# Joining the first-pass weights of layer one from a float16 copy and one shift

## The chip, the core and the metric

The kernel runs on one core of one Trainium2 chip. The engines of that core work at the same time, each through its own list of instructions in order: TensorE (PE, and PEld for its weight loads), VectorE (DVE), ScalarE (ACT), GpSimd (POOL) and SyncE (SP), whose queue issues nearly all DMAs here. They wait for each other through semaphores. The metric is the device time of one execution in microseconds.

## The reference, cut to what matters

Attention over 4 batches with 8 heads, 576 positions and head size 64 (four heads see a local window of 32, four a strided pattern), then two dense layers on the 2304 rows of 512 values:

```python
x = attention(q, k, v)                      # (2304, 512)
r = maximum(x @ moe_w_in, 0)                # (2304, 2048)
x = (s * (r * r) + b) @ moe_w_out           # (2304, 512)
h = x @ moe2_w_in
out = ((h * cos(h)) @ moe2_w_out).astype(float32)
```

The weights come as float64. The chip's engines don't compute in that format, so the kernel takes each weight apart by its bits: it reads the two 32-bit words of a float64, builds a float32 from them, and splits that into a rounded part (hi) and a rest (lo), since TensorE multiplies the format float32r and three products (hi by hi, hi by lo, lo by hi) stand for one float32 product.

## The kernel before

**Stages.** From the start to about 155 us the kernel computes the attention, batch by batch, and beside it the first of two "plain" passes of layer one (PASSES = (5, 3): five chunks of 128 hidden columns, then three). From then on come the second pass and the products of both layers in blocks, up to the end.

**Attention.** A batch is five pairs of heads (two local, two strided, one "rem" for what is left over). For each pair TensorE forms the scores (L649, into `s_ps`; for the first two batches the mask is added by L642), VectorE takes the maximum (L663) and scales it (L665), ScalarE forms the exponentials (L670, four for each of the two halves j), VectorE normalises (L681, L682 and L683, into `part`), TensorE transposes (L696, `t_ps`), ScalarE copies (L707), TensorE multiplies by the values (L742, `o_ps`), and the result is split on ScalarE (L166, `xhi`) and VectorE (L171, `xlo`). In batches after the first, GpSimd does the small L665 and L681. Runs of products into `dummy` (L775) keep TensorE busy while the first pairs go through.

**The first pass.** The functions `mm_h` and `mm_2` multiply x by chunk n of the first weights (`h_ps`, L928), and, after the activation on ScalarE and VectorE (L951 to L957, split into `gh`, `gl`), by chunk n of the second ones (`acc`, L928). A weight chunk (n, k) must be converted first: k is 0 for the first weights and 1 for the second.

**Conversion of the first five chunks.** These ten tiles of 128 x 512 float64 weights are loaded early by `w_early_load` (L299) into the buffers `wearly`, issued from SP's queue between the loads of q, k and v; a buffer that a converted tile has left takes the next tile (`w_next_load`). `convert_ops` gives the list of steps: four on VectorE into the float32 tile `wtmp` (L178 scales the high word, L252 shifts it by 3, L254 ors in the top of the low word, L259 ors in the sign), then the hi part on ScalarE (`w<-wtmp`, L166) and the lo part on VectorE (`w<-wtmp,w`, L171). `bg_step` takes 1.8 steps of that list per step of the attention. The chunks of the second pass (`wraw`, L342) go the same way but have L178's step on ScalarE (L176). All weights that come later in the kernel are converted in another way, by `to_f32`: ScalarE copies the top 16 bits as float16 into `consts` (L200) and VectorE joins them with bits 16 to 47 in one instruction (L201).

**What sets the order.** The Python code gives one program order; a scheduler then places each engine's instructions by the times at which it expects their inputs to be ready, and keeps a few pairs apart where the code says so. So a conversion with fewer steps moves its neighbours on several engines.

Of the kernel before, what the change touches and what calls it, by code (L numbers as in the profile page):

```python
# [9 lines left out]
F32 = mybir.dt.float32  # L10
F32R = mybir.dt.float32r
BF16 = mybir.dt.bfloat16
U32 = mybir.dt.uint32
U16 = mybir.dt.uint16
F16 = mybir.dt.float16
AF = mybir.ActivationFunctionType
ALU = mybir.AluOpType
# [5 lines left out]
P = 128  # L23
NC = DM // P
NF = DFF // P
# [21 lines left out]
FP = PASSES[0]  # L47
# [84 lines left out]
def net(ctx, tc, qkl, qks, rqk, vloc, vstr, rv, wi1, wo1, wp1, wo2, wp2, s, b, out):  # L132
    nc = tc.nc
    wi_raw = wi1.bitcast(U32)
    wo_raw = [x.bitcast(U32) for x in (wo1, wo2)]
    wp_raw = [x.bitcast(U32) for x in (wp1, wp2)]

    const = ctx.enter_context(tc.tile_pool(name="const", bufs=1))
    wp = ctx.enter_context(tc.tile_pool(name="wp", bufs=1))
# [4 lines left out]
    h_p = ctx.enter_context(tc.tile_pool(name="hs", bufs=3))  # L144
# [11 lines left out]
    identb = constb[:, :P]  # L156
    mloc = constb[:, P : P + 4 * LK].rearrange("p (n k) -> p n k", n=4)
    mrem = constb[:, P + 4 * LK :].rearrange("p (n k) -> p n k", n=4)
    sb = const.tile([P, 32], F32, name="sb")
    xhi = const.tile([P, NC, NT], F32R, name="xhi")  # L160
    xlo = const.tile([P, NC, NT], F32R, name="xlo")
    part_p = ctx.enter_context(tc.tile_pool(name="part", bufs=1))
# [2 lines left out]
    def split_hi(dst_hi, src, scale=1.0):  # L165
        nc.scalar.activation(dst_hi, src, AF.Copy, scale=scale)  # L166

    def split_lo(dst_lo, src, hi, scale=1.0):
        if scale != 1.0:
            return nc.vector.scalar_tensor_tensor(dst_lo, src, scale, hi.bitcast(F32), ALU.mult, ALU.subtract)  # L170
        return nc.vector.tensor_tensor(dst_lo, src, hi.bitcast(F32), ALU.subtract)  # L171


    def rebias(t, h, on_act):
        if on_act:
            nc.scalar.activation(t, h.bitcast(F32), AF.Copy, scale=2.0**-112)  # L176
        else:
            nc.vector.tensor_scalar(t, h.bitcast(F32), 2.0**-112, None, ALU.mult)  # L178
# [42 lines left out]
    class Raw:  # L221


        def __init__(self, tile, src):
# [7 lines left out]
            else:  # L232
                self.words = tile[:, :1024]
                nc.sync.dma_start(out=self.words, in_=src)

    wtile, ready = {}, set()
    converted = [None]

    def convert_ops(raws, dst, key):

        tmp = st_p.tile([P, 512], F32, tag="st", name="wtmp")
        ops = []
        o = 0
        on_act = key[0] >= FP
        for raw in raws:
            n = raw.shape[1]
            t = tmp[:, o : o + n]
            tu = t.bitcast(U32)
            lo32, hi32 = raw[:, :, 0], raw[:, :, 1]
            o += n  # L250
            ops.append(lambda t=t, h=hi32: rebias(t, h, on_act))
            ops.append(lambda tu=tu: nc.vector.tensor_scalar(tu, tu, 3, None, ALU.logical_shift_left))  # L252
            ops.append(
                lambda tu=tu, l=lo32: nc.vector.scalar_tensor_tensor(  # L254
                    tu, l, 29, tu, ALU.logical_shift_right, ALU.bitwise_or
                )
            )
            ops.append(
                lambda tu=tu, h=hi32: nc.vector.scalar_tensor_tensor(  # L259
                    tu, h, 0x80000000, tu, ALU.bitwise_and, ALU.bitwise_or  # L260
                )
            )
        ops.append(lambda: split_hi(dst[:, 0, :], tmp))

        def last():
            converted[0] = split_lo(dst[:, 1, :], tmp, dst[:, 0, :])

        if key[0] < 2:
            ops += [lambda: None] * 3
        ops.append(last)  # L270
        ops.append(lambda: ready.add(key))
        if key in raw_at:
            ops.append(lambda: w_next_load(key))
        return ops

    def w_src(n, k, c0, c1):
        src = wo_raw[n // NF][n % NF] if k else wi_raw[n]
        return src[:, 2 * c0 : 2 * c1].rearrange("p (c t) -> p c t", t=2)
# [14 lines left out]
    raws, raw_at = {}, {}  # L293
    to_load = [(n, k) for n in range(2, FP) for k in range(2)]

    def w_early_load(n, k, at):
        raw_at[n, k] = at
        raws[n, k] = raw = wp.tile([P, 512, 2], U32, name="wearly", **at)
        nc.sync.dma_start(out=raw, in_=w_src(n, k, 0, 512))  # L299

    def w_next_load(key):

        if to_load and key != (1, 1):
            w_early_load(*to_load.pop(0), raw_at[key])
# [32 lines left out]
    def w_job(n, k):  # L337

        raws = []
        for c in range(2):  # L340
            raw = st_p.tile([P, 256, 2], U32, tag="st", name="wraw")
            nc.sync.dma_start(out=raw, in_=w_src(n, k, 256 * c, 256 * (c + 1)))  # L342
            raws.append(raw)
        return convert_ops(raws, w_alloc(n, k), (n, k))
# [666 lines left out]
    nc.vector.memset(zeros, 0.0)  # L1011
    warm = zeros.bitcast(BF16)
    nc.vector.memset(sb, 0.0)
    nc.scalar.activation(sb[:, 2:3], sb[:, 3:4], AF.Exp)
    make_identity(nc, ident)
    def keep(m, base, pattern, cm):
# [28 lines left out]
    for what, *arg in FIRST:  # L1045
        if what == "w":
            w_early_load(*arg, dict(tag="w15", bufs=1) if arg[1] else buf0())
        else:
            {"qk": load_qk, "v": load_v, "rq": load_rem_qk, "rv": load_rem_v}[what](0, *arg)

    for n, k in BG_ORDER:
        bg.append(lambda n=n, k=k: convert_ops([raws.pop((n, k))], w_alloc(n, k), (n, k)))
# [3 lines left out]
    while not att.batch_done(0):  # L1056
        next(steps)
        tick()
        if att.n == 3 and (1, 1) not in raws:
            for n, k in SECOND:  # L1060
                w_early_load(n, k, dict(tag="w14", bufs=1))
            nc.sync.dma_start(out=sb[:, 0:1], in_=s.partition_broadcast(P))
            nc.sync.dma_start(out=sb[:, 1:2], in_=b.partition_broadcast(P))
        if normed[0] is not None and (bg_now or att.n >= EARLY_AT[len(BG_ORDER) - len(bg)]):
            prev = converted[0] or normed[0]
            with tc.issue_after(normed[0].ins), tc.issue_after(prev.ins):
                bg_step(EARLY_BG)
        if early < 2 and att.pairs[PRE // 2 + early].stored:
            mm_h(0, early)
            early += 1  # L1070
# [50 lines left out]
    for i in range(14):  # L1121
        k, cp, prev = RING[i % 12]
# [30 lines left out]
    class Temp:  # L1153
# [8 lines left out]
        def set(self, x, y, op=ALU.subtract):  # L1162
            def at(z, i):
                if isinstance(z, Temp):
                    return z.ms[i][1] if len(z.ms) == len(self.ms) else z.ms[0][1][:, self.ms[i][0], :]
                return z[:, self.ms[i][0], :]

            for i, (_, t) in enumerate(self.ms):
                nc.vector.tensor_tensor(t, at(x, i), at(y, i), op)  # L1169
                yield  # L1170
# [101 lines left out]
    for u_, (ly, s_, p) in enumerate(UNITS[:NU2]):  # L1272
        for f in range(2):
# [4 lines left out]
            key = u_, f  # L1278
            if held.get(b_, (None,))[0] == (ly, p):
                key = held[b_][1]  # L1280
# [653 lines left out]
    for u in range(NU2 + 2):  # L1934
# [15 lines left out]
        hs = {}  # L1950
# [165 lines left out]
```

## Time and profile before

| | us |
|---|---|
| Median of 3 runs | 829.58 |
| Lowest and highest | 829.22, 830.01 |
| The profiled execution | 829.99 |
| Span of its trace | 828.2 |
| Busy: PE | 814.7 |
| Busy: DVE | 639.1 |
| Busy: ACT | 588.9 |

The profiled execution is 0.41 us above the median, and 1.8 us of it lie outside the span of the trace. A row of the trace names a line of the kernel, an engine, an operation and its tiles (result<-inputs). "Idle before" is the time in which an engine had nothing running, and the arrow behind it names what ended that wait. Where the engine waited for nothing that the profile shows, the word there is "issue".

### The profile page before, as it was taken

The page shows a single profiled execution, that of the slowest core. Times are in us where ns is not written, and L with a number is a line of the kernel's source. Part 1 is how long each engine was busy: PE and PEld are TensorE (multiplying, and loading weights), DVE is VectorE, ACT ScalarE, POOL GpSimd, SP SyncE. Part 2 cuts the span into 40 slices and gives each one's busy share as a digit, 9 for nine tenths or more (in the row PEclk, how much of TensorE's full clock was granted, in tenths as well). Part 3 has the DMA queues.
Part 4 walks back from the last instruction along what each step waited for, and adds up shares of the span by engine and source line. Part 5 has one row for each costly group of instructions (what it writes and reads, how often), then busy time and mean ns, then how long its engine had stood idle before and what let it go on. Part 6 is the DMA issues. An engine that isn't in the chain of part 4 may idle for free.

```text
span 828.2 us, 15435 instructions
## 1 busy us (share of the span) xinstructions
PE 814.7 (98%) x5545; PEld 731.2 (88%) x5545; DVE 639.1 (77%) x1209; ACT 588.9 (71%) x1237; POOL 20.5 (2%) x74
## 2 busy tenths in 40 slices
PE   8899999999999999999999999999999999999998
PEld 5676777889888999899999999898899999999998
DVE  6898866877668569976766787877758999578985
ACT  7888877668767677777678666667568765589753
POOL 3120000000000000000000000000000000000000
PEclk9999999999999999999999999999999999999999
DMA  9755542587688988996889989899797878974675
GB/s 336 231 192 169 160 125 85 196 287 244 245 306 297 359 313 287 331 322 222 306 290 376 327 290 359 306 307 384 250 351 260 273 251 259 290 251 151 210 248 179
DMA packets 102269, 220.00 MB, mean 266 GB/s; under 512 B 9136, under 2 KB 53424, under 8 KB 102192
## 3 DMA queue, kind: packets, MB, share of 16 engines
q1 hardware_dynamic: 100464, 211.83, 75.0%
q10 hardware_dynamic: 1728, 7.18, 2.6%
q8 instruction: 44, 0.72, 0.3%
q14 instruction: 33, 0.27, 0.1%
HBM read 163.92 MB, written 55.05 MB: 264 GB/s over the span
## 4 chain that ended last, share of the span: by engine, by line
PE 77%; DVE 7%; ACT 2%; issue 1%; DMA 1%; ACTq 0%; DVEq 0%
PE acc L1872 10%; PE acc L928 9%; PE pb L1982 9%; PE pa L1982 9%; PE h_ps L928 9%; PE acc L1681 8%; PE acc L1862 7%; PE acc L1551 6%; PE pa L1551 3%; PE pb L1551 3%; DVE graw L1142 2%; DVE xlo L171 2%; PE pa L1681 1%; PE pb L1681 1%; DVE xt L1169 1%
## 5 line engine op out<-in xcount | busy, mean ns | idle before, releaser
L928 PE MATMUL h_ps<-xhi,w 128*128 128x512 f32 (+1 forms) x320 | 100.9, 377 | 0.2
L928 PE MATMUL acc<-gh,w 128*128 128x512 f32 (+1 forms) x320 | 99.1, 374 | 0.0
L1872 PE MATMUL acc<-gh,w2l 128*128 128x512 f32 (+1 forms) x384 | 84.9, 336 | 0.0
L1982 PE MATMUL pb<-xhi,wfl 128*128 128x384 f32 x268 | 80.1, 339 | 0.4 <-DVE h L1962 0.2
L1982 PE MATMUL pa<-xhi,wfl 128*128 128x384 f32 x268 | 79.6, 337 | 0.0
L166 ACT ACTIVATE xhi<-graw 128x384 fp32r<-128x384 f32 (+1 forms) x84 | 51.3, 629 | 38.4 <-DVE graw L1142 18.3
L928 PEld LDWEIGHTS h_ps<-xhi,w 128*128 128x128 f32 x320 | 58.5, 189 | 11.8 <-ACT w L166 1.1
L928 PEld LDWEIGHTS acc<-gh,w 128*128 128x128 f32 x320 | 58.4, 189 | 10.2 <-ACT gh L166 0.2
L1681 PE MATMUL acc<-xhi,w2m 128*128 128x384 f32 x256 | 67.1, 334 | 0.0
L1872 PEld LDWEIGHTS acc<-gh,w2l 128*128 128x128 f32 x384 | 59.7, 188 | 7.6 <-DMA w2l<-w2s 0.4
L1419 ACT ACTIVATE h<-h 128x768 f32<-128x768 f32 x48 | 40.3, 840 | 29.2 <-DVE h L1962 28.9
L171 DVE TENSOR_TENSOR xlo<-graw,xhi 128x384 fp32r<-128x384 f32 (+1 forms) x84 | 55.0, 686 | 7.5 <-ACT xhi L166 7.5
L1862 PE MATMUL acc<-w2l,gh 128*128 128x512 f32 x192 | 59.7, 390 | 0.0
L928 PE MATMUL h_ps<-xlo,w 128*128 128x512 f32 (+1 forms) x160 | 59.4, 371 | 0.0
L928 PE MATMUL acc<-gl,w 128*128 128x512 f32 (+1 forms) x160 | 59.3, 371 | 0.0
L1551 PE MATMUL acc<-xhi,wfl 128*128 128x384 f32 x196 | 55.2, 335 | 0.1
L171 DVE TENSOR_TENSOR gl<-r,gh 128x512 fp32r<-128x512 f32 (+2 forms) x56 | 40.6, 725 | 16.1 <-ACT gh L1419 8.7
L1982 PEld LDWEIGHTS pb<-xhi,wfl 128*128 128x128 f32 x268 | 49.4, 188 | 3.5 <-DVE h L1962 1.0
L1982 PEld LDWEIGHTS pa<-xhi,wfl 128*128 128x128 f32 x268 | 49.4, 188 | 1.7 <-ACT q L1994 0.4
L1872 PE MATMUL acc<-gl,w2l 128*128 128x512 f32 x192 | 49.0, 335 | 0.0
L1681 PEld LDWEIGHTS acc<-xhi,w2m 128*128 128x128 f32 x256 | 46.4, 188 | 0.0
L1982 PE MATMUL pb<-xlo,wfl 128*128 128x384 f32 x134 | 45.0, 336 | 0.0
(248 smaller groups left out, 2087.4 us busy)
## 6 DMA issues: line engine op xcount, KB each, us to landing
wfl<-wfb SPq DMA_DIRECT2D x68, 512.0 KB, 5.1
wfl<-wfa SPq DMA_DIRECT2D x34, 512.0 KB, 5.7
w2l<-w2s SPq DMA_DIRECT2D x28, 512.0 KB, 5.8
praw<-in_wp_dram SPq DMA_DIRECT2D x22, 512.0 KB, 4.8
oraw<-in_wo_dram SPq DMA_DIRECT2D x22, 512.0 KB, 4.8
w2m<-wsum SPq DMA_DIRECT2D x22, 512.0 KB, 3.8
wfb<-ob SPq DMA_DIRECT2D x21, 512.0 KB, 4.3
w2s<-ow SPq DMA_DIRECT2D x20, 512.0 KB, 4.4
```

The source lines that it names most:

```text
L166: nc.scalar.activation(dst_hi, src, AF.Copy, scale=scale)
L171: return nc.vector.tensor_tensor(dst_lo, src, hi.bitcast(F32), ALU.subtract)
L928: nc.tensor.matmul(*args, **kw)
L1142: return nc.vector.tensor_tensor(d, x, y, op)
L1169: nc.vector.tensor_tensor(t, at(x, i), at(y, i), op)
L1419: return nc.scalar.activation(*args, **kw)
L1551: nc.tensor.matmul(self.bank(v, bi), a, b[:, m, :], start=st and m == 0 and i == 0, stop=m == 1 and i == 2, skip_group_check=True)
L1681: nc.tensor.matmul(self.acc(j, e), w[u][:, wi, c], g[:, u], start=first and i == 0, stop=last and i == 2, skip_group_check=True)
L1862: nc.tensor.matmul(accs[e], g[:, e * P : (e + 1) * P], w[:, wi, :], start=start and i == 0, stop=stop and i == 2, skip_group_check=True,)
L1872: nc.tensor.matmul(o, w[:, wi, e * P : (e + 1) * P], g[:, c : c + o.shape[1]], start=start and i == 0 and (c == 0 or e % 2 == 0), stop=sto ...
L1982: nc.tensor.matmul(pb[bi], a, b[:, m, :], start=st and m == 0 and i == 0, stop=m == 1 and i == 2, skip_group_check=True)
```

## The change

The ten tiles of the first pass's weights now go the way of `to_f32`, but with both steps on VectorE. The load puts the 4,096 bytes of a partition's row at 2 bytes past the buffer's start, so that bits 16 to 47 of every float64 form an aligned 32-bit word. The first new step multiplies the top 16 bits, read as bfloat16, by 0.5 and writes them as float16 into the upper halves of a new tile `tops`, whose lower halves stay zero; the second shifts the middle word right by 13 and ors the two. The value so made is a 256th of the weight, and the factor 256 goes into the two splits, which were plain before. `tops` is one buffer of the pool `hs`, cleared once at the start; `sb` shrinks from 32 to 8 columns. The number of entries in the list stays (two of them do nothing now).

```diff
-    sb = const.tile([P, 32], F32, name="sb")
+    sb = const.tile([P, 8], F32, name="sb")
...
+    tops = h_p.tile([P, 512], F32, tag="hs", name="tops")
...
+        scale = 1.0
+        if key[0] < FP:
+            raw, scale = raws[0], 256.0
+            halves, middles = raw.bitcast(BF16)[:, 4:2052:4], raw[:, 1:1025:2]
+            ops += [
+                lambda: nc.vector.tensor_scalar(tops.bitcast(F16)[:, 1::2], halves, 0.5, None, ALU.mult),
+                lambda: nc.vector.scalar_tensor_tensor(
+                    tmp.bitcast(U32), middles, 13, tops.bitcast(U32), ALU.logical_shift_right, ALU.bitwise_or
+                ),
+                lambda: None,
+                lambda: None,
+            ]
+            raws = []
...
-        ops.append(lambda: split_hi(dst[:, 0, :], tmp))
+        ops.append(lambda: split_hi(dst[:, 0, :], tmp, scale))
...
-            converted[0] = split_lo(dst[:, 1, :], tmp, dst[:, 0, :])
+            converted[0] = split_lo(dst[:, 1, :], tmp, dst[:, 0, :], scale)
...
-        raws[n, k] = raw = wp.tile([P, 512, 2], U32, name="wearly", **at)
-        nc.sync.dma_start(out=raw, in_=w_src(n, k, 0, 512))
+        raws[n, k] = raw = wp.tile([P, 1026], U32, name="wearly", **at)
+        nc.sync.dma_start(out=raw.bitcast(U16)[:, 1:2049], in_=(wo_raw[n // NF][n % NF] if k else wi_raw[n]).bitcast(U16))
...
+    nc.vector.memset(tops, 0.0)
```

The change moves instructions up to about the end of the third batch's first pairs; behind that, all engines have the same order as before. In the rows that follow, lines of the new kernel are up to 15 higher: L677, L679, L684, L695, L696, L697, L710, L721, L942 are L663, L665, L670, L681, L682, L683, L696, L707, L928 of before, and its L251 and L252 are the two new steps.

VectorE in the attention of the first batch, at the conversion of the second tile, before. `sm` holds the maxima and sums, `part_99` the exponentials of a strided pair; `s_ps` and the last two `sm` belong to the "rem" pair:

```order
L254 SCALAR_TENSOR_TENSOR wtmp<-wearly,wtmp 128x512
L683 TENSOR_TENSOR part_99<-part_99,sm 128x256
L681 TENSOR_SCALAR sm<-sm 128x4
L663 TENSOR_REDUCE sm<-s_ps 128x4
L682 RECIPROCAL sm<-sm 128x4
L663 TENSOR_REDUCE sm<-s_ps 128x4
L683 TENSOR_TENSOR part_99<-part_99,sm 128x256
L259 SCALAR_TENSOR_TENSOR wtmp<-wearly,wtmp 128x512
L171 TENSOR_TENSOR xlo<-o_ps,xhi 128x18x12 x2
L665 TENSOR_SCALAR sm<-sm 128x4 x2
```

The same place on VectorE now:

```order
L252 SCALAR_TENSOR_TENSOR wtmp<-wearly,tops 128x512
L695 TENSOR_SCALAR sm<-sm 128x4
L696 RECIPROCAL sm<-sm 128x4
L697 TENSOR_TENSOR part_99<-part_99,sm 128x256
L695 TENSOR_SCALAR sm<-sm 128x4
L677 TENSOR_REDUCE sm<-s_ps 128x4
L696 RECIPROCAL sm<-sm 128x4
L677 TENSOR_REDUCE sm<-s_ps 128x4
L697 TENSOR_TENSOR part_99<-part_99,sm 128x256
L679 TENSOR_SCALAR sm<-sm 128x4 x2
```

The last joining step and the two `xlo` splits no longer stand between the maxima and their scaling. ScalarE a little later, before; the eight exponentials of `part_99` are those of the "rem" pair, `w_534` is the hi part of the second tile:

```order
L166 ACTIVATE xhi<-o_ps 128x18x12 x2
L166 ACTIVATE w_534<-wtmp 128x512
L707 ACTIVATE part_98<-t_ps 128x512
L670 ACTIVATE part_99,sm<-s_ps,sm 128x64 x8
L670 ACTIVATE part_98,sm<-s_ps,sm 128x96 x2
```

The same place on ScalarE now; the first eight exponentials of `part_99` in this piece are the "rem" pair's:

```order
L166 ACTIVATE w_534<-wtmp 128x512
L684 ACTIVATE part_99,sm<-s_ps,sm 128x64
L166 ACTIVATE xhi<-o_ps 128x18x12 x2
L684 ACTIVATE part_99,sm<-s_ps,sm 128x64 x2
L721 ACTIVATE part_98<-t_ps 128x512
L684 ACTIVATE part_99,sm<-s_ps,sm 128x64 x5
L684 ACTIVATE part_98,sm<-s_ps,sm 128x96 x4
```

The hi part has moved ahead of the `xhi` splits; of the "rem" pair's exponentials one now stands ahead of those splits, and two more ahead of the copy of the transposes. TensorE after the first batch, before; `w_534` and `w_661` are the first weights of chunk 1 and the second weights of chunk 0, `part_99` an attention pair of the second batch:

```order
L928 MATMUL h_ps<-xhi,w_534 128x512 x2
L928 MATMUL h_ps<-xlo,w_534 128x512
L928 MATMUL h_ps<-xhi,w_534 128x512
L696 MATMUL t_ps<-consts,part_99 96x128 x4
L928 MATMUL acc<-gh,w_661 128x512 x4
L696 MATMUL t_ps<-consts,part_99 96x128 x4
L928 MATMUL acc<-gl,w_661 128x512
```

The same place on TensorE now; `w_853` are the first weights of chunk 2:

```order
L942 MATMUL h_ps<-xhi,w_534 128x512
L942 MATMUL h_ps<-xlo,w_534 128x512
L942 MATMUL h_ps<-xhi,w_534 128x512 x2
L942 MATMUL h_ps<-xlo,w_534 128x512
L942 MATMUL h_ps<-xhi,w_534 128x512
L942 MATMUL h_ps<-xhi,w_853 128x512
L942 MATMUL h_ps<-xlo,w_853 128x512
L942 MATMUL h_ps<-xhi,w_853 128x512
L710 MATMUL t_ps<-consts,part_99 96x128 x4
L942 MATMUL h_ps<-xhi,w_853 128x512
L942 MATMUL h_ps<-xlo,w_853 128x512
L710 MATMUL t_ps<-consts,part_99 96x128 x4
```

The products of chunk 2 now stand ahead of the transposes of that pair and of the first products into `acc`.

## Rows read from the trace of the kernel before

**Rows 1.** The page: busy time by engine, and shares of the chain of waits.

```profile
PE 814.7 (98%) x5545; PEld 731.2 (88%) x5545; DVE 639.1 (77%) x1209; ACT 588.9 (71%) x1237; POOL 20.5 (2%) x74
...
PE 77%; DVE 7%; ACT 2%; issue 1%; DMA 1%; ACTq 0%; DVEq 0%
```

**Rows 2.** Windows: stretch, length, busy us (instructions) by engine, granted clock, DMA share, GB/s.

```profile
10.00:33.00 23.00, 19.74 (x404) 13.86 (x402) 19.52 (x63) 19.20 (x95) 1.51 (x5) 1.00 0.97 315
33.00:80.00 47.00, 44.99 (x560) 32.62 (x560) 43.33 (x108) 41.83 (x150) 6.76 (x18) 1.00 0.53 176
80.00:120.00 40.00, 38.45 (x483) 30.41 (x482) 29.98 (x81) 30.92 (x117) 2.21 (x10) 1.00 0.48 145
120.00:160.00 40.00, 39.97 (x373) 32.29 (x372) 28.79 (x75) 29.44 (x98) 2.07 (x8) 1.00 0.35 123
```

**Rows 3.** Waits of PE from 10 to 120 us: total us, times, longest.

```profile
PE t_ps L696 <- DVE part L683: 1.5, 3, 0.8
...
PE s_ps L649 <- issue: 0.4, 1, 0.4
```

**Rows 4.** Groups on DVE: count, busy us, mean ns of one, idle before.

```profile
L201 DVE SCALAR_TENSOR_TENSOR ta<-praw,consts 128x512 uint32<-128x512 uint32 x20 | 13.8, 691 | 9.4 <-ACT consts L200 9.2
...
L171 DVE TENSOR_TENSOR w<-wtmp,w 128x512 fp32r<-128x512 f32 x16 | 11.0, 686 | 0.0
...
L170 DVE SCALAR_TENSOR_TENSOR ow<-tw,ow 128x512 fp32r<-128x512 f32 x12 | 8.3, 691 | 7.9 <-ACT ow L166 7.9
...
L254 DVE SCALAR_TENSOR_TENSOR wtmp<-wearly,wtmp 128x512 uint32<-128x512 uint32 x10 | 6.8, 685 | 0.0
...
L259 DVE SCALAR_TENSOR_TENSOR wtmp<-wearly,wtmp 128x512 uint32<-128x512 uint32 x10 | 6.8, 682 | 0.0
...
L252 DVE TENSOR_SCALAR wtmp<-wtmp 128x512 uint32<-128x512 uint32 x10 | 4.1, 412 | 0.0
...
L178 DVE TENSOR_SCALAR wtmp<-wearly 128x512 f32<-128x512 f32 x10 | 4.1, 416 | 0.0
```

**Rows 5.** Timeline of DVE at the start: start us, length, instruction, idle before.

```profile
5.46 1.02 DVE L663 TENSOR_REDUCE sm<-s_ps 128x4 f32<-128x384 f32 x2 [3.29 <-PE s_ps L649]
```

**Rows 6.** Timeline of DVE at the second tile.

```profile
20.30 0.43 DVE L252 TENSOR_SCALAR wtmp<-wtmp 128x512 uint32<-128x512 uint32 x1
...
22.84 0.69 DVE L259 SCALAR_TENSOR_TENSOR wtmp<-wearly,wtmp 128x512 uint32<-128x512 uint32 x1
23.44 0.66 DVE L171 TENSOR_TENSOR xlo<-o_ps,xhi 128x216 fp32r<-128x216 f32 x2
24.02 0.23 DVE L665 TENSOR_SCALAR sm<-sm 128x4 f32<-128x4 f32 x2
```

**Rows 7.** Timeline of ACT at the same place.

```profile
21.97 0.59 ACT L166 ACTIVATE xhi<-o_ps 128x216 fp32r<-128x216 f32 x2 [0.50 <-PE o_ps L742]
23.56 0.63 ACT L166 ACTIVATE w<-wtmp 128x512 fp32r<-128x512 f32 x1 [0.99 <-DVE wtmp L259]
24.57 0.31 ACT L670 ACTIVATE part<-s_ps,sm 128x64 f32<-128x64 f32 x1
```

**Rows 8.** Timeline of PE: its four longest waits between 20 and 80 us.

```profile
27.72 0.41 PE L696 MATMUL t_ps<-consts,part 128*128 128x128 f32 x2 [1.55 <-ACT part L670]
...
31.82 0.44 PE L742 MATMUL o_ps<-part,part 64*64 64x32 f32 x17 [1.63 <-issue]
...
58.26 0.44 PE L696 MATMUL t_ps<-consts,part 128*128 128x128 f32 x2 [0.39 <-DVE part L683]
...
75.67 0.61 PE L696 MATMUL t_ps<-consts,part 128*96 128x128 f32 x4 [0.75 <-DVE part L683]
```

**Rows 9.** DMA issues, 154 to 159 us (in place), 159 to 161 us (shifted): KB, us to landing.

```profile
oraw<-in_wo_dram SPq DMA_DIRECT2D x1, 512.0 KB, 3.2
...
praw<-in_wp_dram SPq DMA_DIRECT2D x1, 512.0 KB, 3.2
```

**Rows 10.** Waits of ACT from 33 to 80 us.

```profile
ACT w L166 <- DVE wtmp L259: 1.7, 2, 1.3
```

## The prediction, as put on record before the changed kernel ran

> **What bounds the kernel now.** I read the page first: TensorE is busy for 98% of the span, and the chain of waits that ends last is PE for 77% of it [rows 1]. So only what shortens or lengthens TensorE's idle time can move the end, as long as its own work stays. It does: the change adds and removes no matrix product, and the list of PE's instructions is the same set in a slightly other order. The second view is the table by windows. TensorE idles for 23.00 - 19.74 = 3.26 us between 10 and 33 us (the attention of the first batch), for 47.00 - 44.99 = 2.01 us up to 80 us (where the remaining early tiles are converted), for 1.55 us up to 120 us, and for 0.03 us in the 40 us behind that [rows 2]. The granted clock is 1.00 throughout. All conversions that the change touches lie in the first two of these windows. What it can win is therefore at most 3.26 + 2.01 + 1.55 = 6.8 us, 0.8% of the time, although VectorE, which it relieves, is busy for 19.52 of the 23 us and 43.33 of the 47 us there. That VectorE is nearly full does not yet make it the bound: ScalarE is as full (19.20 and 41.83 us) and keeps all its work.
>
> The third view is who PE waits for. Four waits make up most of the idle time up to 80 us: 1.55 us for exponentials at 27.72, 1.63 us inside one run of value products at 31.82, and 0.39 and 0.75 us for normalised scores at 58.26 and 75.67 [rows 8]. The waits for L683 sum up to 1.5 us in three, the third of them behind 80 us, and a shorter wait of 0.4 us has no releaser [rows 3].
>
> **What the change costs and saves on VectorE.** A tile took 416 + 412 + 685 + 682 + 686 = 2,881 ns of VectorE [rows 4]. It will take the first new step, the joining step and the scaled lo split. The joining step and the scaled split exist already, at 691 ns each. The first new step has no row of its own on VectorE: it reads 16-bit values with gaps and writes 16-bit values with gaps. From below it is bounded by 412 ns, the price of a one-input step on 512 values, and from above by 691 ns, that of a step with two inputs. I take 416 ns, since L178 is a multiplication by a constant that also reads every second word and is the nearest row. Then a tile costs 416 + 691 + 691 = 1,798 ns and sheds 1,083 ns (808 ns at the dear end); ten tiles shed 10.8 us (8.1). Three tiles lie in the first window and seven in the second. The zeroing of `tops` is one more step at the start: at most 691 ns, and VectorE idles for 3.29 us there before the first maximum [rows 5], so it costs nothing.
>
> **Where that lands.** (a) The wait of 1.55 us. The transposes at 27.72 need the "rem" pair's exponentials, which begin on ScalarE at 24.57 [rows 7]. They need the scaled maxima (L665), which VectorE gave at 24.02, behind the joining step at 22.84 (0.69 us) and the two `xlo` splits at 23.44 (0.66 us) [rows 6]. They also stand on ScalarE behind the hi part of the weights, which began at 23.56 after a wait of 0.99 us for that same joining step [rows 7]. The changed order takes all of this away: the joining step is earlier by a whole step, since L252 with its 0.43 us [rows 6] is gone, the splits now follow the scaling, and the hi part is ahead of the `xhi` splits. L665 comes 24.02 - 22.84 = 1.2 us earlier from its two vanished predecessors alone. Of the eight exponentials one now stands ahead of the `xhi` splits and three ahead of the copy, so the splits (0.59 us) and the copy come in among them: the last exponential ends some 1.2 us earlier, not more. TensorE's wait falls from 1.55 to some 0.35 us: **-1.2 us**. Bounds: -1.55 if all goes, and -0.3 if the `xhi` splits, which now wait for L665 too, hold ScalarE up as long as the 0.99 us did.
>
> (b) The wait of 1.63 us at 31.82 lies inside a run of 40 products whose inputs were all there, and the profile shows no releaser. The run keeps its length and its place behind the same number of instructions. I leave it: **0**, bounds -1.63 and +0.3.
>
> (c) Waits for L683 between 33 and 80 us: 0.39 + 0.75 = 1.14 us. L683 queues on VectorE behind conversions and splits. VectorE sheds 7 x 1.08 = 7.6 of its 43.33 us there. The second of the two lies behind the last early tile, so I take the first wholly and 0.3 us of the second: **-0.7 us**, bounds -1.14 and 0.
>
> (d) Behind 80 us every engine has the same instructions in the same order, VectorE is at 29.98 of 40 us, and nothing that it does there is shorter: **0**, bounds -0.5 and +0.5.
>
> (e) ScalarE: the hi split has a scale now, and its count is the same; **0**. GpSimd: its list has two neighbours exchanged; **0**.
>
> (f) The loads. SP issues the same number of DMAs with the same bytes. Some of the ten weight loads are issued a place or two earlier, ahead of a load of q, k or v, because their buffers are free earlier; the loads that they pass serve pairs one turn or more further on, and none of PE's waits named above is for a load, so **0**. That a row lands 2 bytes off is seen in this kernel's later loads: 512 KB took 3.2 us in place and 3.2 us shifted [rows 9]. **0**, bounds 0 and +0.3, since that stretch was quiet and the first window has the DMA engines at 0.97 [rows 2].
>
> A rule speaks against that. The Trainium skill, DMA: Bandwidth & Descriptors, section "How a descriptor splits into AXI transactions", says that a transaction must begin on a 256-byte boundary, so that a run that begins off one costs an extra transaction. If it held on the side that is written, a row of 4,096 bytes would take 17 for 16, an estimate of 6% more, 0.2 us on each such load of 3.2 us; with three tiles in the first window the sum would be 0.6 us higher at most by it, and by the row it is unchanged. The trace's 3.2 us on either side does not agree with it.
>
> The sum is -1.2 - 0.7 = -1.9 us. Against the profiled execution that is 829.99 - 1.9 = 828.1; the median of the runs stands 0.41 us below that execution, so **827.7 us**.
>
> **The rivals.** *Handed back.* VectorE isn't what paces the first batch: ScalarE is as full, and its work stays. Now both halves' transposes stand in one row on PE, so the first waits for the second's norm no less than before, and the wait re-forms. For it: ScalarE at 19.20 of 23 us. Against it: two of ScalarE's waits there are VectorE's doing. Then only some -0.3 us is left: 829.3 (828.6 to 830.2).
>
> *More.* The wait without a releaser goes too, because the loads around it have moved, and all of (c) goes, with a further 0.5 us of short waits: -1.55 - 1.63 - 1.14 - 0.5 = -4.8, so 824.8 (824.6 to 826). For it: TensorE idles for 6.8 us in all. Against it: nothing in the change reaches that wait directly.
>
> *Slower.* In the changed order TensorE meets the products of chunk 2 before the transposes of the second batch, and of later chunks likewise. TensorE runs in order: if such a weight isn't split yet, the transposes queue behind it, and with them the exponentials' copies, values and everything that ScalarE and VectorE do for that pair. The longest wait for a weight's joining step is 1.3 us [rows 10]. If three of the seven tiles of that stretch cost as much, that is +3.9, less the 1.2 of (a): +2.7 us, 832.3 (830.5 to 833.5). It is slower than before from two such waits on, since 2.6 us outweigh the 1.9 won. Against it: the weights are ready a step earlier than before.
>
> *Not what it says.* If the first new step ran at 691 ns, a tile would still shed 0.81 us; (a) would lose at most 0.28 us. That lies within the forecast's own range.
>
> **How the numbers follow.** Forecast (827.7, own range 826.5 to 829.2, from the ends of (a) and (c)): 0.52. Handed back: 0.20. More: 0.17. Slower: 0.11. The range from 824.6 to 830.2 leaves out the slower case and little else. A difference of 0.2%, 1.7 us, is about what a measurement of this kernel can tell from none, so faster means below 827.9 and slower above 831.2. The forecast lies by its size to 0.31 below that and to 0.21 within; "more" is faster; "handed back" is 0.02 faster and 0.18 the same; "slower" is 0.09 beyond and 0.02 within. Together: faster 0.50, same 0.41, slower 0.09.
>
> **What would show it.** In the changed profile: a group of ten on VectorE for the first new step at 0.41 to 0.42 us, the joining steps at 0.69; VectorE's busy time down by 8 to 11 us; in the window from 10 to 33 us TensorE idle for under 2.2 us, with no wait of over 0.5 us for exponentials; the 1.6 us wait inside the value products still there; the landing of the weight loads unchanged. If TensorE's idle time up to 33 us stays at 3 us or more, (a) is wrong and the stage is paced by ScalarE; if new waits of `h_ps` for `w` stand between 33 and 80 us, the order is the cause; if the end moves by more than TensorE's idle time up to 120 us does, the whole argument is wrong.

## The result, and the profile after

The changed kernel took 835.39 us in the median (833.72 to 836.17, six runs), the kernel before 829.80 us beside it. The ratio is 1.0062, 95% interval [1.0046, 1.0077]: slower by 0.6%, where 827.7 us and a range up to 830.2 had been forecast. A second measurement beside other runs gave 1.0041 [1.0025, 1.0057]. All later ratios are to runs of the kernel before that were taken beside them.

The page of the changed kernel (span 832.9 us): busy time by engine, then the chain of waits by engine.

```profile
PE 819.8 (98%) x5545; PEld 737.0 (88%) x5545; DVE 632.6 (76%) x1190; ACT 588.8 (71%) x1237; POOL 19.3 (2%) x74
...
PE 82%; DVE 3%; ACT 0%; issue 0%; DVEq 0%
```

Beside [rows 1], VectorE is relieved as meant (639.1 to 632.6 us). TensorE, with the same 5,545 products, is busy for 5.1 us more, and the span is 4.7 us longer. So the loss lies in the time that products take, not in idle time. The windows of the changed kernel (stretch, length, busy us by engine, granted clock, DMA share, GB/s) say the same:

```profile
10.00:33.00 23.00, 20.01 (x407) 14.23 (x406) 19.46 (x61) 20.43 (x102) 2.37 (x6) 1.00 1.02 339
33.00:80.00 47.00, 45.03 (x560) 33.97 (x558) 37.68 (x95) 40.95 (x149) 4.88 (x18) 0.96 0.56 176
80.00:120.00 40.00, 38.12 (x484) 30.09 (x477) 28.38 (x75) 30.25 (x113) 1.98 (x9) 1.00 0.46 135
120.00:160.00 40.00, 40.00 (x397) 32.19 (x387) 28.71 (x75) 29.34 (x100) 2.07 (x8) 1.00 0.35 116
```

TensorE's idle time is 2.99, 1.97, 1.88 and 0.00 us, 6.84 in sum, for 6.85 us in [rows 2]. Two things are new. The granted clock is 0.96 of full between 33 and 80 us, where it was 1.00. And the loss goes on where the change touches nothing: laid product by product beside the trace of before, the changed kernel is 0.9 us late at 150 us, 2.1 late at 265, still 2.1 at 440, and 4.7 late at its last product (829.08 for 824.41 us). The first 0.7 us of that are there at 10 us already, ahead of every changed product (last section); 3.7 us come behind 150 us. The next view says why: groups of matrix products (line, output<-inputs, shapes, count | busy us, mean ns of one | idle before). First the kernel before, then the changed one.

```profile
L1681 PE MATMUL acc<-xhi,w2m 128*128 128x384 f32 x256 | 67.1, 334 | 0.0
L1862 PE MATMUL acc<-w2l,gh 128*128 128x512 f32 x192 | 59.7, 390 | 0.0
L928 PE MATMUL h_ps<-xlo,w 128*128 128x512 f32 x128 | 50.3, 393 | 0.0
```

```profile
L1696 PE MATMUL acc<-xhi,w2m 128*128 128x384 f32 x256 | 67.9, 338 | 0.0
L1877 PE MATMUL acc<-w2l,gh 128*128 128x512 f32 x192 | 60.0, 392 | 0.0
L942 PE MATMUL h_ps<-xlo,w 128*128 128x512 f32 x128 | 51.4, 402 | 0.0
```

Products of the same size take 2 to 9 ns more each (5 of the 9 come from two slow products, of 0.63 and 0.78 us, in a stretch shown further down), the last ones of the program (L1681) among them, hundreds of microseconds behind the last changed instruction and at a granted clock of 1.00. What the change still alters there is where the tiles lie. `sb` lost 96 bytes, so `xhi` moved from byte 3328 of a partition to 3232 and `xlo` likewise; `wearly` grew from 4,096 bytes to 4,128 with padding in each of four buffers, which later weights use too, so three of the weights' buffers moved by -96, -64 and -32 bytes, two stayed, and the rest of them, `gh`, `gl`, the temporary tiles and the partial sums moved by +32.

### The profile page after: what moved, and what is told of

Its sections match the earlier page's. It is cut to its first block, busy times and chain, and to the rows that moved or that the text cites. A ratio compares the mean times of both kernels' runs of the same rounds, so it can differ in the third digit from the quotient of the medians.

```text
span 832.9 us, 15415 instructions
## 1 busy us (share of the span) xinstructions
PE 819.8 (98%) x5545; PEld 737.0 (88%) x5545; DVE 632.6 (76%) x1190; ACT 588.8 (71%) x1237; POOL 19.3 (2%) x74
## 4 chain that ended last, share of the span: by engine, by line
PE 82%; DVE 3%; ACT 0%; issue 0%; DVEq 0%
PE acc L1696 12%; PE acc L1887 10%; PE acc L942 9%; PE pb L1997 9%; PE pa L1997 9%; PE h_ps L942 9%; PE acc L1877 8%; PE acc L1566 6%; PE pa L1566 4%; PE pb L1566 3%; PE pa L1696 1%; PE pb L1696 1%; DVE xt L1184 1%; PE o_ps L756 1%; DVE h L1977 0%; PE t_ps L710 0%
## 5 line engine op out<-in xcount | busy, mean ns | idle before, releaser
L942 PE MATMUL h_ps<-xhi,w 128*128 128x512 f32 (+1 forms) x320 | 101.8, 381 | 0.1
L942 PE MATMUL acc<-gh,w 128*128 128x512 f32 (+1 forms) x320 | 99.8, 375 | 0.0
L942 PEld LDWEIGHTS h_ps<-xhi,w 128*128 128x128 f32 x320 | 59.1, 190 | 11.3 <-DVE w L170 0.3
L942 PEld LDWEIGHTS acc<-gh,w 128*128 128x128 f32 x320 | 58.4, 188 | 10.6
L942 PE MATMUL h_ps<-xlo,w 128*128 128x512 f32 (+1 forms) x160 | 60.4, 378 | 0.0
L942 PE MATMUL acc<-gl,w 128*128 128x512 f32 (+1 forms) x160 | 59.2, 370 | 0.0
L1997 PE MATMUL pa<-xlo,wfl 128*128 128x384 f32 x134 | 45.2, 338 | 0.0
```

The source lines that it names most:

```text
L942: nc.tensor.matmul(*args, **kw)
L1997: nc.tensor.matmul(pb[bi], a, b[:, m, :], start=st and m == 0 and i == 0, stop=m == 1 and i == 2, skip_group_check=True)
```

## Theories

**A:** the addresses set the pace of the products. **B:** the new steps, their order, their waits or the clock's fall behind them make the loss. A third question is where the forecast gain of 1.9 us went.

## Experiments on the addresses

The first four: the kernel before with all tiles shifted together; with the inputs alone shifted; with all but the inputs shifted; and the changed kernel with the old addresses.

```
b_sb24:  -    sb = const.tile([P, 32], F32, name="sb")
         +    sb = const.tile([P, 24], F32, name="sb")
b_x32:   as b_sb24, and behind xlo
         +    gap = const.tile([P, 8], F32, name="gap")
b_w32:   that gap alone, sb as before
a_left:  the changed kernel with
         +    sb = const.tile([P, 32], F32, name="sb")
         +    halves, middles = raw.bitcast(BF16)[:, 2:2048:4], raw[:, 0:1024:2]
         +    raw = wp.tile([P, 1024], U32, name="wearly", **at)
         +    nc.sync.dma_start(out=raw.bitcast(U16)[:, 0:2047], in_=(...).bitcast(U16)[:, 1:2048])
```

> The kernel before with the tile sb cut from 32 to 24 columns and nothing else changed: every tile behind it stands 32 bytes lower (xhi 3296 for 3328, xlo 40160 for 40192, the weights' tiles from 77024 for 77056), so all the large tiles move from multiples of 64 bytes to 32 behind one, which is where the change puts most of them. Theory A (addresses: the matmuls take longer from such tiles, as h_ps from xhi 401 to 406 ns and from xlo 393 to 402 in the trace of the changed kernel): 833 to 835 us, with those means again and no fall of the granted clock at 33 us. Theory B (the change's own steps, waits and the clock's fall behind them): 829.6 us.

> The kernel before with sb cut to 24 columns and a tile of 32 bytes behind xlo: only xhi and xlo stand 32 bytes lower (3296, 40160), all else where it was. Theory A with the inputs as the cause: the first pass's h_ps products slow as in the changed kernel (406 and 402 ns) and the whole 832 to 835 us. Theory A with the weights' tiles as the cause: near 829.6. Theory B: 829.6.

> The kernel before with a tile of 32 bytes behind xlo: xhi and xlo stand where they were (multiples of 64), every tile behind them (weights, gh, partial sums) 32 bytes higher. Theory A with the weights' tiles as the cause: 832 to 835 us, acc<-w2l,gh 392 for 390 ns; with the inputs as the cause: near 829.6, h_ps at 401 and 393 ns. Theory B: 829.6.

> The changed kernel with its two new steps, its order and its tops, but with the addresses of the kernel before: sb has 32 columns again, and the weights are loaded 2 bytes to the left (the double's first 2 bytes are left out) instead of 2 to the right, so wearly keeps 4,096 bytes. Theory A: the matmuls' means are back (h_ps 401 and 393 ns) and the time is 829.5 to 831 us: what is left is the shift of the first 150 us, up to 0.9 us, and less if the predicted 1.9 us shows. Theory B: 834 to 836 us, as the changed kernel, with the granted clock at 0.50 from 33 to 36 us.

| run | inputs moved | weights moved | gh, gl and the rest moved | median us | ratio, 95% interval |
|---|---|---|---|---|---|
| b_sb24 | -32 | -32 | -32 | 829.75 | 0.9991 [0.9982, 1.0000] |
| b_x32 | -32 | 0 | 0 | 831.86 | 1.0017 [1.0007, 1.0028] |
| b_w32 | 0 | +32 | +32 | 832.83 | 1.0031 [1.0019, 1.0042] |
| a_left | 0 | 0 | 0 | 829.88 | 0.9995 [0.9985, 1.0005] |

Theory A fell in the form that I had written down: every tile 32 bytes off a multiple of 64 costs nothing (b_sb24). But b_x32 and b_w32, in which the inputs stand 32 bytes further from the weights, are slower with the steps of before, and the changed kernel with the old addresses loses nothing. So what counts is not where the tiles lie but how they lie to one another. B is out for most of the loss.

The second four put that to a number: the kernel before with the changed kernel's addresses, and with the inputs at three other distances.

```
b_lay:   -        raws[n, k] = raw = wp.tile([P, 512, 2], U32, name="wearly", **at)
         +        wide = wp.tile([P, 1026], U32, name="wearly", **at)
         +        raws[n, k] = raw = wide[:, :1024].rearrange("p (c t) -> p c t", t=2)
         and sb of 8 columns
b_x64:   sb of 16 columns, gap of 16 behind xlo
b_x96:   sb of 8 columns, gap of 24
b_x128:  sb of 8 columns, gap of 32
```

> The kernel before, its steps and order untouched, with the addresses of the changed kernel: sb of 8 columns and the weights' tiles wearly of 1,026 words, of which 1,024 are used (xhi 3232, the four of these tiles at 76960, 81088, 85216 and 93440, all behind them 32 bytes higher than before). Theory A (where the tiles stand against each other sets the matmuls' pace): 833.5 to 835.5 us, with the pace of the changed kernel (h_ps from xhi 406 and from xlo 400 ns or more, pa and pb from xhi 339 and 341 ns) and the loss growing to the end. Theory B (the changed steps are needed for the loss): 829.5 to 830.5 us.

> The kernel before with xhi and xlo 64 bytes lower (sb of 16 columns and a tile of 64 bytes behind xlo) and all else in place. If what counts is the distance of the inputs to the weights' tiles in steps of 64 bytes: as before, 830. If any change of that distance costs: 831.5 to 833 us, as with 32 bytes (831.9).

> The kernel before with xhi and xlo 96 bytes lower (sb of 8 columns and a tile of 96 bytes behind xlo), all else in place. If the distance counts modulo 64 bytes: 831.9, as with 32 bytes. If modulo 128 or more: another time, anywhere from 830 to 835 us.

> The kernel before with xhi and xlo 96 bytes lower and everything behind them 32 bytes higher, so 128 bytes further apart, as in the changed kernel for all tiles but three of the weights'. If those three tiles make the loss of the changed kernel: near 830. If the distance of 128 bytes makes it: 833.5 to 835.5 us, as in the changed kernel.

| run | inputs to weights, against before | median us | ratio, 95% interval |
|---|---|---|---|
| b_lay | as in the changed kernel | 833.70 | 1.0046 [1.0033, 1.0059] |
| b_x64 | 64 bytes further | 834.68 | 1.0056 [1.0043, 1.0068] |
| b_x96 | 96 bytes further | 832.47 | 1.0039 [1.0024, 1.0054] |
| b_x128 | 128 bytes further | 833.77 | 1.0050 [1.0036, 1.0064] |

b_lay has none of the change's steps and loses 3.6 us, where the changed kernel lost 5.6 and, measured again, 3.9: the addresses alone make most of the loss. None of the distances tried (32, 64, 96 and 128 bytes) is free, so it is neither a matter of 64 nor of 128 bytes. b_x64 is slower than either of its expectations said. In the changed kernel five of the weights' buffers, not three as the text of b_x128 has it, stand less than 128 bytes further from the inputs (0, 32, 64, 96 and 96); b_x128 shows that these aren't needed for the loss.

Two more runs ask which distance it is, and whether a larger step is free: one moves the inputs by 2,048 bytes, one moves only what lies behind the weights.

```
b_x2048: consts declared behind xlo, in place of ahead of sb
b_g32:   +    gap_p = ctx.enter_context(tc.tile_pool(name="gap", bufs=1))   (between the pools wp and g)
         +    gap = gap_p.tile([P, 8], F32, name="gap")
```

> The kernel before with consts moved behind xlo: xhi and xlo stand 2,048 bytes lower (1280, 38144), the weights and all behind them where they were. If the distance of inputs and weights counts within a row of some power of two up to 2,048 bytes: 829.5 to 830.5, as before. If before's distance is good by itself alone: 832 to 835 us.

> The kernel before with a tile of 32 bytes behind the weights' pool: inputs and weights stand where they were, and the rest (gh, gl, the temporary tiles, qk, the partial sums) 32 bytes higher. If only the distance of the inputs to the weights counts, which are read together by the matmuls: products from xhi and xlo unchanged (h_ps 401 and 393, pa 337), at most those from gh and gl longer, 829.8 to 831. If the distance to what ScalarE and VectorE read and write counts: 831.5 to 834.5, with h_ps at 404 or more.

b_x2048: 830.08 us, 0.9999 [0.9988, 1.0011]. b_g32: 833.44 us, 1.0040 [1.0028, 1.0052]. Both expectations for b_g32 missed: the time is that of the second, the products are those of the first. The same groups as above, for b_sb24, b_x64 and b_g32:

```profile
L1681 PE MATMUL acc<-xhi,w2m 128*128 128x384 f32 x256 | 67.1, 334 | 0.0
L1862 PE MATMUL acc<-w2l,gh 128*128 128x512 f32 x192 | 59.7, 390 | 0.0
L928 PE MATMUL h_ps<-xlo,w 128*128 128x512 f32 x128 | 50.3, 393 | 0.0
```

```profile
L1682 PE MATMUL acc<-xhi,w2m 128*128 128x384 f32 x256 | 67.7, 337 | 0.0
L1863 PE MATMUL acc<-w2l,gh 128*128 128x512 f32 x192 | 59.5, 389 | 0.0
L929 PE MATMUL h_ps<-xlo,w 128*128 128x512 f32 x128 | 50.8, 396 | 0.0
```

```profile
L1683 PE MATMUL acc<-xhi,w2m 128*128 128x384 f32 x256 | 67.1, 334 | 0.0
L1864 PE MATMUL acc<-w2l,gh 128*128 128x512 f32 x192 | 60.7, 395 | 0.0
L930 PE MATMUL h_ps<-xlo,w 128*128 128x512 f32 x128 | 50.5, 394 | 0.0
```

All moved together: these lines don't change by a nanosecond. Inputs moved: the products that read `xhi` or `xlo` beside a weight are slower, those of `gh` and `w2l` in this line are not. What lies behind the weights moved: the products of `gh` and `w2l` are slower, and those of the inputs stay within 1 ns. In these lines a product is slower when its own two tiles have come to stand differently to one another.

Other groups don't fit. The products of L1872 are slower in b_x32, where only the inputs moved and none of their own tiles did. Before and b_x32:

```profile
L1872 PE MATMUL acc<-gl,w2l 128*128 128x512 f32 x96 | 37.7, 393 | 0.0
L1872 PE MATMUL acc<-gl,w2l 128*128 128x256 f32 x96 | 26.7, 278 | 0.0
```

```profile
L1873 PE MATMUL acc<-gl,w2l 128*128 128x512 f32 x96 | 38.4, 400 | 0.0
L1873 PE MATMUL acc<-gl,w2l 128*128 128x256 f32 x96 | 27.1, 282 | 0.0
```

In b_g32, where one of their tiles moved, the same two took 390 and 282 ns. Products of `xhi` beside `xhi` (L1681), which moved together, went from 334 to 336 ns in b_x32, and those of L928 on 256 columns became faster there (`h_ps<-xhi,w`, 282 to 280). So more counts than the distance within one product; whether it is the tiles of neighbouring products, or what the other engines read and write at that time, is open. The mechanism inside TensorE or the memory is not shown by any view here. That 2,048 bytes are free speaks for a pattern that repeats within a power of two, but no run here tells how soon.

The last of this kind asks which of the change's two edits it was.

```
a_left8: a_left with sb of 8 columns, as in the change
```

> The changed kernel with wearly of 4,096 bytes (loads 2 bytes to the left) but sb of 8 columns, as in the change: all tiles behind sb stand 96 bytes lower, at the same distances from one another. If distances alone count: as a_left, 829 to 830.5, with h_ps at 402 ns and pa at 337. If the smaller sb has a part of its own: 831.5 or more.

828.79 us, 0.9990 [0.9974, 1.0005], a little below the expected range. The smaller `sb` moves everything together and is innocent. The 8 bytes that widened `wearly`, 32 with padding in each of four buffers and so up to 128 in all, made the loss.

## Experiments on the clock and the gain

In the changed kernel the granted clock falls to 0.50, the lower of its two levels (1.2 GHz), at 33 us and is back at 36.3. Three stretches of it:

```profile
31.00:33.00 2.00, 0.90 (x22) 0.85 (x22) 1.04 (x3) 1.33 (x9) 1.03 (x3) 0.97 1.04 407
33.00:36.00 3.00, 3.00 (x11) 2.37 (x10) 2.41 (x8) 2.46 (x13) 0.23 (x1) 0.50 0.39 153
36.00:38.00 2.00, 2.00 (x12) 1.24 (x11) 0.89 (x3) 1.33 (x6) 0.02 (x1) 0.93 0.03 11
```

Ahead of it TensorE had idled twice, as its timeline shows:

```profile
28.10 0.41 PE L710 MATMUL t_ps<-consts,part 128*128 128x128 f32 x2 [1.13 <-DVE part L697]
...
32.10 0.48 PE L756 MATMUL o_ps<-part,part 64*64 64x32 f32 x17 [1.57 <-issue]
```

In the kernel before two waits as long stand at the same places [rows 8] and the clock stays at 1.00. In a_left it falls as well; there the values that before began at 31.82 began at 31.14, 0.68 us ahead, and the next but one pair's at 44.61 for 43.52, 1.09 behind: 1.77 us lost in the stretch. a_left8, with the same products in the same order, kept the clock and lost 0.45 us there. So the next experiment fills the second wait with six dummy products behind the scores at 28 us; two controls put the same dummies into the kernel before and into the changed kernel with its own addresses.

```
a_fill:  a_left with
         -FILL = {1: 6, 2: 5, 3: 5, 4: 5, 5: 5}
         +FILL = {1: 6, 2: 5, 3: 5, 4: 5, 5: 5, 6: 6}
b_fill:  the same line in the kernel before
w_fill:  the same line in the changed kernel
a_again: the changed kernel once more
```

> The changed kernel with the addresses of before (a_left) and six dummy products more behind the scores at 28 us, which fill TensorE's wait of 1.3 us before the rest of the values at 31.1 us. If that wait is what the granted clock falls behind: it stays at 1.00, the values at 44.6 us come 1.5 to 2 us earlier. Theory 'given back': the end is not earlier than that of a_left all the same (829.4 to 830.2), since waits at 98 and 113 us take it. Theory 'the clock hid the gain': 827.5 to 828.5.

> The changed kernel, unaltered, beside the others of this call. Its ratio was 1.0062 [1.0046, 1.0077]; the kernel before with the same addresses gave 1.0046 [1.0033, 1.0059]. If the addresses are the whole loss and the changed steps cost nothing beside them: 1.004 to 1.006, 833.5 to 835. If the fall of the granted clock at 33 us adds its part there: 1.006 to 1.008, 835 to 836.5.

> The kernel before with the same six dummy products more behind the scores at 28 us, nothing else. If the 2.0 us that a_fill gained come from the changed steps, with the clock kept: 829.5 to 830.5, the clock being 1.00 there already and the wait of 1.63 us being long enough for six products. If the dummies alone gain them: 827.5 to 828.5.

> The changed kernel, with its own addresses, and the six dummy products. If addresses and clock are separate parts that add up: the addresses cost the 3.6 us that they cost in the kernel before, the steps gain 2.0: 831.2 to 832.5. If the addresses' loss needs the clock's fall or the reverse: 830 or below, or 834.

| steps | addresses | dummies | run | median us | ratio, 95% interval |
|---|---|---|---|---|---|
| before | before | yes | b_fill | 831.60 | 1.0021 [1.0012, 1.0031] |
| changed | before | no | a_left | 829.88 | 0.9995 [0.9985, 1.0005] |
| changed | before | yes | a_fill | 828.06 | 0.9976 [0.9965, 0.9987] |
| changed | changed | no | a_again | 833.98 | 1.0041 [1.0025, 1.0057] |
| changed | changed | yes | w_fill | 832.23 | 1.0030 [1.0021, 1.0039] |

a_fill is faster than both kernels, by 0.24% against the kernel before, and it stands where the forecast stood, though with dummies that the forecast didn't have. Its timeline of TensorE and its clock at the place:

```profile
27.79 0.41 PE L710 MATMUL t_ps<-consts,part 128*128 128x128 f32 x2 [1.13 <-DVE part L697]
...
29.45 1.14 PE L789 MATMUL dummy<-consts 128*128 128x384 bf16 x6
...
31.53 0.66 PE L756 MATMUL o_ps<-part,part 64*64 64x32 f32 x23 [0.53 <-issue]
```

```profile
32.00:34.00 2.00, 1.17 (x14) 0.81 (x10) 1.48 (x4) 2.00 (x14) 0.62 (x2) 1.00 0.77 304
```

The dummies stand in the wait, 0.53 us of it is left, and the clock stays. How far each kernel had come by the same value products of the attention, with the clock fallen (a_left), not fallen (a_left8) and with dummies (a_fill):

```profile
102.35 0.69 PE L756 MATMUL o_ps<-part,v 64*64 64x54 f32 x32
```

```profile
101.81 0.69 PE L756 MATMUL o_ps<-part,v 64*64 64x54 f32 x32
```

```profile
100.58 0.69 PE L756 MATMUL o_ps<-part,v 64*64 64x54 f32 x32
```

The kernel before has them at 102.65. a_left8 and a_fill were 0.97 and 0.36 us later than these two at 10 us already (last section), so against their own starts the three are 0.30, 1.81 and 2.43 us ahead of the kernel before. Between a_left and a_left8, which differ in the clock's fall, stand 1.5 us; the dummies came out 0.6 us ahead of the kept clock. These are single executions, and others scatter as much: with the steps of before, and at distances that cost nothing, b_sb24 has these products 0.3 us behind the kernel before and b_x2048 1.0 us ahead, against their own starts. b_fill rules out that the dummies alone make the gain: it is slower than before, and slower than both of its expectations. Its profiled execution lost 1.2 of its 1.8 us by a fall of the clock at 11.5 us, ahead of the added dummies, and the wait that they were to fill didn't occur in it; whether they cost it anything is open. w_fill against a_fill gives the price of the addresses again, 0.54% or 4.5 us. So the parts roughly add up: about -2 us for the steps and dummies, +3.6 to +4.5 for the addresses.

What the fall costs is read from single executions. Among the eleven runs of a_left the mean granted clock does not sort the times (five at 1.00: 829.0 to 830.8; six at 0.997 to 0.999: 829.0 to 831.2), since other things scatter by as much. That the clock's fall is the cause of the whole difference between a_left and a_fill is therefore likely, not shown.

## Why the prediction was wrong, by its own steps

**The step that failed** is the first: only TensorE's idle time can move the end, "as long as its own work stays. It does". The list of products stayed; what one of them takes did not. The prediction read the widened `wearly` and the smaller `sb` as memory, and priced the 2 bytes by which the load is shifted, but not the 32 to 128 bytes by which the other tiles came to stand further from the inputs. It had said that the whole argument is wrong if the end moves by more than TensorE's idle time up to 120 us does; the idle time hardly moved, and the end moved by 4.7 us.

**The prices on VectorE** held for the two dear steps; the first new step is 10% dearer than the row that stood for it. The groups of the changed kernel:

```profile
L252 DVE SCALAR_TENSOR_TENSOR wtmp<-wearly,tops 128x512 uint32<-128x512 uint32 x10 | 6.8, 682 | 0.1
...
L170 DVE SCALAR_TENSOR_TENSOR w<-wtmp,w 128x512 fp32r<-128x512 f32 x10 | 6.8, 686 | 0.2
...
L251 DVE TENSOR_SCALAR tops<-wearly 128x512 f16<-128x512 bf16 x10 | 4.6, 459 | 1.5 <-DMA wearly<-in_wi_dram 1.5
```

459 ns for 416, so a tile costs 1,827 ns for 1,798 and sheds 1,054. The sum over VectorE's instructions falls by 9.6 us, with 0.5 us more for `tops` in it; the page's busy time, which counts overlapping instructions once, falls by 6.5, where 8 to 11 were forecast.

**(a)** -1.2 forecast. The wait for exponentials is gone, but 1.13 us for the norm (L697) stands in its place [rows 8]. The first half's transposes come 1.8 us earlier in a_left (25.88 for 27.72 us); the second half's now follow them at once and wait. What is left shows at the scores behind both halves, before and in a_left:

```profile
28.60 0.89 PE L649 MATMUL s_ps<-qk 64*64 64x96 f32 x32
```

```profile
28.09 0.89 PE L663 MATMUL s_ps<-qk 64*64 64x96 f32 x32
```

That is 0.5 us, and 0.5 in the changed kernel, a_left8 and a_fill too, against their own starts. The sign was right, the size less than half, and TensorE's idle time up to 33 us stayed at 2.99 us, where under 2.2 was forecast.

**(b)** was forecast at 0 with wide bounds: 1.63 us before, 1.30 to 1.57 in the changed kernels without dummies. In the ten kernels with the order of before it ran from nothing to 1.92 us. The traces say what this wait goes with. Queue q8 of the profile, "instruction", brings 16 KB of the program at a time. In all eleven traces that have the wait, TensorE goes on 1.3 to 1.6 us after such a load has ended (30.44 us in the kernel before, 29.72 in a_left); in the six that lack it the load ended by 29.5 us. With the six dummies ahead, the wait stands six products earlier in its run (17 products ahead of it in a_fill, 23 in a_left), so it hangs on a place in TensorE's list of instructions. It is very likely a wait for the program itself. When that load comes differs from one execution to the next (with the steps of before it ended between 28.5 and 31.6 us), and with it the time at which TensorE goes on.

**(c)** -0.7 forecast. At 76 us, where the order becomes that of before again, a_left8 is 2.3 us ahead against its own start. Only 0.75 us of that is idle time (5.27 to 4.52 us from 10 us on); the products themselves took 1.5 us less (59.23 us busy; with the steps of before 60.77, and 60.57 and 60.96 in b_sb24 and b_x2048) in the new order, a term that the prediction didn't have. By 102 us a_left8 has lost 0.5 us of it again, with a wait for the norm at 98 us of 0.72 for 0.39 us before.

The sum of (a) to (c), -1.9, stands beside -1.8 (a_left8) and -2.4 (a_fill) in the profiled executions, where clock and addresses are kept. With these terms that is luck: the one large term is not half of what was forecast, and what replaced it is not idle time. In the medians only a_fill shows the gain (2.0 us); a_left and a_left8 gained 0.5 and 1.3 us, with intervals that hold no change. **(d)** Behind 102 us a_fill keeps its lead to the last product, 822.45 for 824.41 us. **(f)** The loads that land 2 bytes off show no price: among the DMA issues of the first 40 us the median from issue to landing is 7.7 and 10.6 us for the two kinds of `wearly`, 8.4 and 10.0 before.

**The rivals.** "Slower" was given 832.3 us for another reason, new waits of `h_ps` for `w`; there is none in the changed trace. "Handed back" was right about (a): the wait re-formed for the norm, which it had given a chance of 0.20. Its time also fits a_left (829.88 us), where the clock's fall may have eaten the rest of the gain; the prediction had read the granted clock of 1.00 as given and had no term for it.

## What to carry to other kernels

A tile that grows by a few bytes moves all that is allocated behind it, and here that cost more than the change could win: compare the addresses of both builds, and keep the distances between the tiles that matrix products read (a load shifted to the other side kept them here). When products of one form and size change their mean time far behind the last moved instruction, look beyond the schedule. Where a change only moves idle time of TensorE about, look at the granted clock of the stretch too, since an idle time that went unpunished before may not stay so.

## What the runs showed of the hardware

Most groups of products of the same form and size took 0.5 to 1.8% longer when the inputs had been shifted by 32 to 128 bytes against the other tiles (`acc<-xhi,w2m`: 336 to 338 ns for 334), and not for a common shift of 32 or 96 bytes, nor for one of 2,048.

The granted clock fell to 0.50 for about 3 us behind waits of 1.1 to 1.9 us in some executions (the changed kernel, a_left, and with the steps of before b_x96) and stayed at 1.00 behind waits as long in others (before, a_left8). The Trainium skill, TensorE: Matmul & The Clock Gate, section "What's actually happening", says that the window in which activity is judged runs freely and isn't reset when a kernel starts; the runs fit that and don't show it.

The first products after the start took up to 1.8 times as long in some executions, with the steps of before (b_x2048) as with the changed ones, though the granted clock reads 1.00 there. The kernel before, then a_left8:

```profile
4.09 0.48 PE L642 MATMUL s_ps<-consts 128*128 128x384 bf16 x2
```

```profile
4.09 0.80 PE L656 MATMUL s_ps<-consts 128*128 128x384 bf16 x2
```

At 10 us such executions are up to 1.0 us late, half of what this change was about.
